# The weight sums of a Strassen product moved from VectorE to GpSimd, in a fused attention and MLP kernel

## The chip, the core and the metric

The kernel runs on one core of a Trainium2 chip. The metric is the device time of one launch in microseconds; lower is better. Engines are named as the profile names them: PE is TensorE's matmul, PEld its weight load, DVE is VectorE, ACT is ScalarE, POOL is GpSimd, SP is SyncE.

## The reference

Attention with a sliding window of 128 and a linear bias per head, over 8 batches, 8 heads, 576 positions and a head size of 64. Its output, as 4608 tokens of 512 columns, goes through two matrix products with a squared ReLU between them.

```
rel   = pos[:, None] - pos[None, :]
mask  = (rel >= 0) & (rel < 128)
s     = where(mask, scale * q @ k.T - slope[h] * |rel|, -1e9)
x     = (softmax(s) @ v)            as [4608, 512]
h     = x @ w_in                    w_in  [512, 2048]
out   = (relu(h) ** 2) @ w_out      w_out [2048, 512], float32
```

## The kernel before, in words

**Attention** is worked off in blocks of 128 keys, five to a batch, the last of 64 (40 blocks, counted here from 0, so that block 14 has 64 rows). For each block POOL issues three loads that also cast to bf16: k and q into a slot of `kq` (a ring of 4) and v into a slot of `vt` (a ring of 6). A slot is loaded again only when its last reader is done. For blocks up to 11 PE turns k and q; from block 12 on SP does it with a transposing DMA, kqT<-kq (L461, L463). PE then makes the scores (ps_s, L533 and L552), ACT the exponential (E, L598), DVE the mask (P, L609), PE the product with v (pv, L639), DVE the division (x, L672), and x is turned into `xT`, a ring of four groups of 512 tokens. The scores of blocks 14 and 15 are one step of PE.

**The MLP** takes the tokens in nine groups of 512. Group 0 is plain. Groups 0 and 1 form h by plain products (L745); groups 2 to 8 form h by Strassen's method in the form of Winograd, seven products of halves in place of eight, in four units of 512 columns of w_in each (`fast_unit`, L820). That needs four sums of w_in per unit, `w_sum`, which are formed once (`weight_sums`, L383 to L394) and used by all later groups, and four sums of the tokens per group. The second matrix product of groups 1 to 8 is formed the same way in seven products (`product`, L975), on sums of g and of w_out. In the last group its last product is done in two halves of 128 tokens each, so that the first can be added and stored while the second is still on PE (`halves`, L970, L1010 to L1022).

**The order of the work** is set by a planner (`Plan.order`). Each task has a cost on each engine that may do it, a key and what it depends on. The planner goes through time; of the tasks that could start soonest on an engine it takes the one with the lowest key. An engine then executes its list in this order and waits where something is not yet there. `SPREAD` (L1099) moves the keys by random draws: a seed, the largest move, and the share of the tasks that are moved (a negative share moves the loads).

Of the kernel before, what the change touches and what calls it, by code (L numbers as in the profile page):

```python
# [12 lines left out]
ALU = mybir.AluOpType  # L13
# [188 lines left out]
def kernel(  # L202
    ctx: ExitStack, tc: tile.TileContext, q, k, v, moe_w_in, moe_w_out, out
):
    nc = tc.nc
# [11 lines left out]
    FCB = d_ff // 128  # L217
    NG = NT // 512
# [41 lines left out]
    def overlap(e):  # L260
# [88 lines left out]
    t_win = [None] * 4  # L349
# [33 lines left out]
    def weight_sums(n, key):  # L383
        w = w_in_sb.rearrange("p (c k) (j r f) -> p c r k j f", c=2, r=2, f=128)
        a11, a12, a21, a22 = (w[:, c, r, :, 2 * n:2 * n + 2] for r in range(2) for c in range(2))
        s1, s2, s3, s4 = (w_sum[:, i, :, 2 * n:2 * n + 2] for i in range(4))
        last = None
        for o, a, b, op in ((s1, a21, a22, ALU.add), (s2, s1, a11, ALU.subtract),
                            (s3, a11, a21, ALU.subtract), (s4, a12, s2, ALU.subtract)):
            def emit(o=o, a=a, b=b, op=op):  # L390
                for k in range(2):
                    nc.vector.tensor_tensor(o[:, k], a[:, k], b[:, k], op=op)
# [333 lines left out]
    g_slots, g_sq, t_read = {}, {}, {}  # L726
# [215 lines left out]
    KEEP = {}  # L942
    BOTH = (2, 5)

    def left(g, what, j):
        if what == "s2":
            return s_slots[g][1].tile[:, j]
        if what in ("s1", "s4"):
            return s_slots[g][0].tile[:, ("s1", "s4").index(what), j]
        a11, a12, a21, a22 = quarters(g, j, 1)  # L950
        return {"a11": a11, "a12": a12, "s3": a21, "a22": a22}[what][:, 0]

    def right(what, j):
        if what[0] == "t":
            return w_mix[:, int(what[1]) - 1, j]
        return w_out_sb[:, 2 * j + int(what[1]) - 1, (int(what[2]) - 1) * 256:int(what[2]) * 256]

    def product(g, i, key):
        what, by, where = PRODUCTS[i]
        if i == 0:  # L960
            KEEP[g] = {"bank": [[Slot("o")] * 2, [Slot("o")] * 2, [Slot("o"), Slot("o")] if g == NG - 1 else [Slot("o")] * 2],
                       "last": None, "t": [None] * 3,
                       "s1": Slot("s1"), "u2": Slot("u2"), "x1": Slot("x1")}
        kp = KEEP[g]
        bank = kp["bank"][where]
# [4 lines left out]
        for j, t in ([(j, t) for t in range(2) for j in range(FCB // 2)] if halves  # L970
                     else [(j, t) for j in range(FCB // 2) for t in range(2)]):
                def emit(j=j, t=t):
                    if opens and j == 0 and (t == 0 or apart):
                        bank[t].tile = bank_tile(bank[t], "o")
                    nc.tensor.matmul(bank[t].tile[:, t * 256:(t + 1) * 256],  # L975
                                     left(g, what, j)[:, t * 128:(t + 1) * 128], right(by, j),
                                     start=opens and j == 0 and (t == 0 or apart), stop=j == FCB // 2 - 1,
                                     skip_group_check=True)
                new = j == 0 and t == 0
                here = [bank[t]] if opens and j == 0 and (t == 0 or apart) else []  # L980
                end = i == 6 and j == FCB // 2 - 1 and t == 1
                if halves and j == 0 and t == 1:
                    half_done = last
# [4 lines left out]
                last = plan.add({"PE": mm(256)}, key(i * 16 + 2 * j + t), emit,  # L988
                                [last, (t_wmix if by[0] == "t" else t_wout)[j // 2], kp["t"][where] if new else None] + needs,
                                here, [g_slots[g], s_slots[g][0]] if end else [s_slots[g][1]] if i == 1 and j == FCB // 2 - 1 and t == 1 else [])  # L990
        kp["last"] = last
        k = key(i * 16 + 15)

        def f32(tag, sl, n):
            sl.tile = work.tile([128, 512], FP32, tag=tag, bufs=n, name=tag)
            return sl.tile

        free = [bank[0]] if i in (2, 5, 6) else []
        if i in (0, 1, 2, 3, 5):
            so = {0: kp["s1"], 1: kp["u2"], 3: kp["x1"]}.get(i) or Slot("osb")  # L1000
            done_ = last
            if i == 1:
                def into():
                    nc.vector.tensor_tensor(bank[0].tile, bank[0].tile, kp["s1"].tile, op=ALU.add)
                done_ = plan.add({"DVE": dve(512)}, k, into, [last, kp["from", "s1"]], [], [kp["s1"]])

            def keep():
                copy(te, f32(so.tag, so, plan.bufs[so.tag]), bank[0].tile)
            te = plan.add({"ACT": act(512), "DVE": dve(512)} if i in BOTH else {"ACT": act(512)}, k, keep, [done_], [so], free)
        elif halves:  # L1010
            for t, dep in ((0, half_done), (1, last)):
                so = Slot("osb")

                def plus(t=t, so=so):
                    nc.vector.tensor_tensor(f32("osb", so, plan.bufs["osb"])[:, 0:256], bank[t].tile[:, t * 256:t * 256 + 256],
                                            kp["u2"].tile[:, t * 256:t * 256 + 256], op=ALU.add)
                te = plan.add({"DVE": dve(256)}, k, plus, [dep, kp["from", "u2"]], [so], [bank[t], kp["u2"]])

                def store(t=t, so=so):
                    r0 = g * 512 + t * 128  # L1020
                    nc.sync.dma_start(out[r0:r0 + 128, 256:512], so.tile[:, 0:256])
                plan.add({"SP": 350.0}, k, store, [te], [], [so], dma=1040.0)  # L1022
            return
        else:
            so = Slot("osb")
            add = kp[{4: "x1", 6: "u2"}[i]]

            te = None
            for lo, hi in ((0, 256), (256, 512)) if apart else ((0, 512),):
                def plus(lo=lo, hi=hi):  # L1030
                    if lo == 0:
                        f32(so.tag, so, plan.bufs[so.tag])
                    nc.vector.tensor_tensor(so.tile[:, lo:hi], bank[lo // 256].tile[:, lo:hi], add.tile[:, lo:hi], op=ALU.add)
# [35 lines left out]
    key = 0  # L1069
# [5 lines left out]
    for g in range(NG):  # L1075
# [27 lines left out]
    shift = dict.fromkeys(work_of + load_of, 0.0)  # L1103
# [53 lines left out]
```

## Time and profile before

| | |
|---|---|
| runs shown, us | 291.15, 291.99, 292.82 (median 291.99) |
| the profiled execution, us | 291.18 |
| its span, first to last instruction | 289.2 us |
| granted TensorE clock | 1.00 |
| PE busy | 281.6 us, 97% |
| DVE busy | 256.1 us, 89% |
| ACT busy | 229.1 us, 79% |
| POOL busy | 107.6 us, 37% |

The time of an execution is a little longer than its span, 291.18 against 289.2 us. Busy time of PE is the time in which matmuls run; they overlap, so that a matmul's own duration (273 ns for 256 columns) is longer than the step from one to the next. In a row of the timeline the columns are start, duration, engine, line, operation, destination and source and, in brackets, idle time before it and what ended it. In a list of waits they are the sum, the count and the longest. In the table of stretches they are the stretch, its length, busy time and instructions of PE, PEld, DVE, ACT and POOL, the granted clock, the share of the DMA engines and GB/s.

### The profile page before, as it was taken

To read this page: it belongs to the slowest core of one execution; us is meant where nothing else is said; L and a number is where in the kernel's file an instruction comes from. 1 tells how busy PE (TensorE), PEld (TensorE's weight loads), DVE (VectorE), ACT (ScalarE), POOL (GpSimd) and SP (SyncE) were. 2 spreads that over 40 slices of the span, in tenths; PEclk is the share of its full clock that TensorE was granted. 3 is DMA by queue.
4 is the path that set the end of the run, shared out by engine and by line. 5 is a ranking of instruction groups with operands and counts; after the bars stand their busy time and mean duration, and the time that the engine had idled before them with its cause. 6 is when DMAs were issued, how large, how long until landed. Compare 5 with 4: busy or idle time off the path is not lost.

```text
span 289.2 us, 9480 instructions
## 1 busy us (share of the span) xinstructions
PE 281.6 (97%) x3869; PEld 239.2 (83%) x3869; DVE 256.1 (89%) x625; ACT 229.1 (79%) x470; POOL 107.6 (37%) x134
## 2 busy tenths in 40 slices
PE   8899999999999999999999999999999999999995
PEld 6788878865788888888988888888888888888884
DVE  6876879999798999998999999989999988998823
ACT  6659888995489985999899989898879888588420
POOL 8958676944672516332634245332000000000000
PEclk9999999999999999999999999999999999999999
DMA  9999999999999999999999999999234101201223
GB/s 135 160 179 174 172 180 186 155 126 208 191 191 141 150 126 192 161 161 110 226 158 126 127 197 157 164 177 158 37 101 70 47 20 61 86 0 39 74 75 109
DMA packets 165867, 38.36 MB, mean 133 GB/s; under 512 B 153024, under 2 KB 165312, under 8 KB 165824
## 3 DMA queue, kind: packets, MB, share of 16 engines
q0 software_dynamic: 114704, 18.10, 92.3%
q1 hardware_dynamic: 50064, 19.41, 35.8%
q8 instruction: 30, 0.49, 0.7%
q10 hardware_dynamic: 1056, 0.26, 0.4%
q14 instruction: 13, 0.11, 0.1%
HBM read 36.70 MB, written 9.44 MB: 160 GB/s over the span
## 4 chain that ended last, share of the span: by engine, by line
PE 88%; POOL 4%; DMA 3%; DVE 2%; ACT 1%; issue 0%; DVEq 0%
PE o L975 33%; PE f L820 30%; PE h L745 8%; PE pv L639 6%; PE o L1054 5%; DMA w_in_sb<-in_moe_w_in_dram 3%; PE ps_s L533 3%; POOL kq L429 2%; PE ps_s L552 2%; POOL vt L429 1%; PE tp L483 1%; POOL w_in_sb L360 1%; PE xp L698 1%; DVE rt L854 1%; DVE g L869 0%
## 5 line engine op out<-in xcount | busy, mean ns | idle before, releaser
L429 POOL DMA_DIRECT2D vt<-in_v_dram x40 | 34.1, 854 | 66.5 <-PE pv L639 58.1
L598 ACT ACTIVATE E<-ps_s 128x384 bf16<-128x384 f32 (+2 forms) x114 | 50.5, 508 | 8.6 <-PE ps_s L533 8.6
L975 PEld LDWEIGHTS <-g 128*128 128x128 bf16 x512 | 49.1, 98 | 6.0
L820 PEld LDWEIGHTS <-w_sum 128*128 128x128 bf16 x448 | 43.1, 97 | 6.3 <-issue 0.5
L609 DVE TENSOR_TENSOR P<-E,masks 128x1024 bf16<-128x1024 bf16 (+1 forms) x67 | 43.5, 656 | 2.5 <-ACT E L598 1.6
L429 POOL DMA_DIRECT2D kq<-in_k_dram x39 | 33.2, 851 | 24.9 <-DMA kqT<-kq 17.5
L975 PEld LDWEIGHTS <-S 128*128 128x128 bf16 x384 | 36.6, 98 | 4.5 <-issue 0.4
L848 ACT ACTIVATE rt<-f 128x512 bf16<-128x512 f32 x56 | 33.2, 600 | 6.8 <-PE f L820 6.6
L975 PE MATMUL o<-w_out_sb,g 128*128 128x256 bf16 x256 | 38.3, 273 | 0.0
L975 PE MATMUL o<-w_mix,g 128*128 128x256 bf16 x256 | 37.2, 273 | 0.0
L745 PE MATMUL h<-xT,w_in_sb 128*128 128x128 bf16 (+1 forms) x384 | 35.3, 237 | 1.2 <-issue 0.6
L975 PE MATMUL o<-w_mix,S 128*128 128x256 bf16 x256 | 36.1, 273 | 0.2 <-ACT E L598 0.2
L820 PEld LDWEIGHTS <-w_in_sb 128*128 128x128 bf16 x336 | 31.8, 97 | 4.4
L820 PE MATMUL f<-xT,w_in_sb 128*128 128x256 bf16 x224 | 34.6, 273 | 0.0
L429 POOL DMA_DIRECT2D kq<-in_q_dram x39 | 33.4, 857 | 2.6 <-PE h L745 1.3
L871 ACT ACTIVATE g<-rt 128x512 bf16<-128x512 bf16 x52 | 32.6, 634 | 1.7 <-DVE rt L859 0.9
L820 PE MATMUL f<-xT,w_sum 128*128 128x256 bf16 x224 | 33.5, 272 | 0.2 <-DVE rt L854 0.2
L672 DVE TENSOR_TENSOR x<-pv,rec 128x256 bf16<-128x256 f32 (+1 forms) x80 | 33.0, 415 | 0.4
L820 PE MATMUL f<-T,w_sum 128*128 128x256 bf16 x224 | 32.1, 273 | 0.0
L639 PE MATMUL pv<-vt,P 128*128 128x65 bf16 x576 | 30.8, 193 | 0.9 <-DVE P L609 0.9
L639 PEld LDWEIGHTS <-P 128*128 128x128 bf16 x576 | 25.7, 97 | 6.1 <-DVE P L609 2.0
L745 PEld LDWEIGHTS <-w_in_sb 128*128 128x128 bf16 x384 | 26.7, 98 | 3.7 <-issue 1.0
(78 smaller groups left out, 504.1 us busy)
## 6 DMA issues: line engine op xcount, KB each, us to landing
out_dram<-osb SPq DMA_DIRECT2D x35, 256.0 KB, 3.7
vt<-in_v_dram POOLq DMA_DIRECT2D x32, 128.0 KB, 5.5
kq<-in_k_dram POOLq DMA_DIRECT2D x31, 128.0 KB, 6.0
kq<-in_q_dram POOLq DMA_DIRECT2D x31, 128.0 KB, 6.3
w_out_sb<-in_moe_w_out_dram POOLq DMA_DIRECT2D x4, 512.0 KB, 9.6
w_in_sb<-in_moe_w_in_dram POOLq DMA_DIRECT2D x6, 256.0 KB, 7.9
kq<-in_k_dram POOLq DMA_DIRECT2D x8, 64.0 KB, 5.7
kq<-in_q_dram POOLq DMA_DIRECT2D x8, 64.0 KB, 6.2
```

The costliest lines, as they stand in the source:

```text
L429: nc.gpsimd.dma_start(o, src[b, :, kb * 128:kb * 128 + n, :].rearrange("h s d -> s h d"))
L533: nc.tensor.matmul(sl.tile[lo:lo + 64, at:at + w], k[rows, c, unit:unit + 64], own[rows, C + c, q0:q0 + w], start=True, stop=True)
L598: nc.scalar.activation(o, src, AF.Exp, bias=0.0, scale=scale)
L609: nc.vector.tensor_tensor(Pt[sP.idx][:, hs, p0:2, 0:n], e, masks[:, hs, p0:2, 0:n], op=ALU.mult)
L639: nc.tensor.matmul(slot_v.tile[:, hi * (D + 1):(hi + 1) * (D + 1)], Pt[sP.idx][:, place(h), part, :], vt[s_in[mk, "v"].idx][:, h, :], star ...
L672: nc.vector.tensor_tensor(xt[sx.idx][0:n, hf * 256:(hf + 1) * 256].rearrange("p (h e) -> p h e", h=4), pv[0:n, :, 0:D], srec.tile[0:n, :]. ...
L745: nc.tensor.matmul(slot.tile[:, f * w:(f + 1) * w], w_in_sb[:, cc, (fc + f) * 128:(fc + f + 1) * 128], xT[:, cc, g * 512 % RING + lo:g * 5 ...
L820: nc.tensor.matmul(bank[name].tile[:, jj * 256:jj * 256 + 256], w, m, start=opens and jj == 0 and k == 0, stop=k == 1, skip_group_check=True)
L848: nc.scalar.activation(srt.tile, bank[name].tile, AF.Relu, bias=0.0, scale=1.0)
L871: nc.scalar.activation(o, i, AF.Square)
L975: nc.tensor.matmul(bank[t].tile[:, t * 256:(t + 1) * 256], left(g, what, j)[:, t * 128:(t + 1) * 128], right(by, j), start=opens and j == ...
L1054: nc.tensor.matmul(bank.tile, g_slots[g].tile[:, fc, t * 128:(t + 1) * 128], w_out_sb[:, fc], start=fc == 0, stop=fc == FCB - 1)
```

## The change

The sixteen sums of w_in leave DVE and go to POOL. On DVE each was two instructions of 256 columns (one for each k); on POOL each is one of 512. Their cost for the planner is 1250 ns each. They stand in POOL's list between the loads, where the planner puts them. Products five and seven of the last group open three banks instead of two: tokens 0 to 127, and tokens 128 to 255 in two pieces of 128 columns. The last product is worked off piece by piece, with an addition and a store for each. `SPREAD` has two draws in place of eleven.

```
-                {"h": 3, "o": 3, "a": 4, "f": 5, "t": 3})
+                {"h": 3, "o": 3, "a": 4, "f": 5, "t": 3, "z": 1})
...
             def emit(o=o, a=a, b=b, op=op):
-                for k in range(2):
-                    nc.vector.tensor_tensor(o[:, k], a[:, k], b[:, k], op=op)
-            last = plan.add({"DVE": 2 * dve(256, 2)}, key, emit, [t_win[n][-1], last, t_read[1][0]])
+                nc.gpsimd.tensor_tensor(o, a, b, op=op)
+            last = plan.add({"POOL": 1250.0}, key, emit, [t_win[n][-1], last, t_read[1][0]])
...
-            KEEP[g] = {"bank": [[Slot("o")] * 2, [Slot("o")] * 2, [Slot("o"), Slot("o")] if g == NG - 1 else [Slot("o")] * 2],
+            KEEP[g] = {"bank": [[Slot("o")] * 2, [Slot("o")] * 2, [Slot("o"), Slot("o"), Slot("z")] if g == NG - 1 else [Slot("o")] * 2],
...
+        parts = [(0, 0, 256), (1, 0, 128), (1, 128, 256)] if apart else [(0, 0, 256), (1, 0, 256)]
...
+        for j, x in ([(j, x) for x in range(len(parts)) for j in range(FCB // 2)] if halves
+                     else [(j, x) for j in range(FCB // 2) for x in range(len(parts))]):
+                t, lo, hi = parts[x]
...
+                    nc.tensor.matmul(bank[x].tile[:, t * 256 + lo:t * 256 + hi],
+                                     left(g, what, j)[:, t * 128:(t + 1) * 128], right(by, j)[:, lo:hi],
...
-            for t, dep in ((0, half_done), (1, last)):
+            for x, (t, lo, hi) in enumerate(parts):
...
-                    nc.sync.dma_start(out[r0:r0 + 128, 256:512], so.tile[:, 0:256])
+                    nc.sync.dma_start(out[r0:r0 + 128, 256 + lo:256 + hi], so.tile[:, 0:hi - lo])
...
-            for lo, hi in ((0, 256), (256, 512)) if apart else ((0, 512),):
+            for x, (lo, hi) in enumerate(((0, 256), (256, 384), (384, 512)) if apart else ((0, 512),)):
...
-    SPREAD = ((78, 3, 1), (425, 16, 0.01), (451, 8, 0.01), (463, 8, 0.03), (537, 3, 0.1), (602, 1.5, -0.15),
-              (705, 3, 0.03), (1454, 16, 0.03), (1463, 3, -0.15), (1578, 3, 0.03), (1611, 3, 0.01))
+    SPREAD = ((9072, 3, 1), (9274, 8, 0.03))
```

Three places show how the lists move. The first is POOL's list from the loads of block 12 on (its k and q go to kq_71, its v to vt_75; the following blocks go to kq_72, kq_73, kq_74 and kq_71 again). Before:

```order
L429 DMA kq_71<-in_q_dram 128x8x64
L429 DMA vt_75<-in_v_dram 128x8x64
L429 DMA kq_72<-in_k_dram 128x8x64
L429 DMA kq_72<-in_q_dram 128x8x64
L429 DMA vt_76<-in_v_dram 128x8x64
L429 DMA kq_73<-in_k_dram 64x8x64
L429 DMA kq_73<-in_q_dram 64x8x64
L429 DMA kq_74<-in_k_dram 128x8x64
L429 DMA kq_74<-in_q_dram 128x8x64
```

And now:

```order
L428 DMA kq_71<-in_q_dram 128x8x64
L428 DMA vt_75<-in_v_dram 128x8x64
L391 TENSOR_TENSOR w_sum<-w_in_sb 128x2x256 x2
L391 TENSOR_TENSOR w_sum<-w_sum,w_in_sb 128x2x256
L428 DMA vt_76<-in_v_dram 128x8x64
L428 DMA kq_72<-in_k_dram 128x8x64
L428 DMA kq_72<-in_q_dram 128x8x64
L391 TENSOR_TENSOR w_sum<-w_in_sb 128x2x256
L391 TENSOR_TENSOR w_sum<-w_sum,w_in_sb 128x2x256
L428 DMA kq_73<-in_k_dram 64x8x64
L428 DMA kq_73<-in_q_dram 64x8x64
```

Three sums stand ahead of block 13's loads and two more ahead of block 14's. Up to q of block 16 there are twelve, and the last of the sixteen stands behind v of block 20.

The second place is DVE's list where the sums of g for group 1 (S, from the rows of g) stand beside the later sums of w_in. Before:

```order
L934 TENSOR_TENSOR S_1577<-S,g 128x1024
L392 TENSOR_TENSOR w_sum<-w_in_sb,w_sum 128x256 x2
L443 COPY xT<-xp 128x4x128
L934 TENSOR_TENSOR g<-g 128x4x256
L392 TENSOR_TENSOR w_sum<-w_in_sb 128x256 x2
L934 TENSOR_TENSOR S<-g,S_1577 128x1024
L392 TENSOR_TENSOR w_sum<-w_sum,w_in_sb 128x256 x2
L609 TENSOR_TENSOR P_85<-E_90,masks 128x1024
```

And now:

```order
L933 TENSOR_TENSOR S_1595<-S,g 128x1024
L442 COPY xT<-xp 128x4x128
L933 TENSOR_TENSOR g<-g 128x4x256
L933 TENSOR_TENSOR S<-g,S_1595 128x1024
L608 TENSOR_TENSOR P_85<-E_90,masks 128x1024 x2
```

The sums of w_in are gone, and the rest closes up.

The third place is the end of DVE's list, the additions of the last group (x and u are kept parts, osb is what is stored). Before:

```order
L1004 TENSOR_TENSOR o<-o,s_5951 128x512
L443 COPY osb<-o 128x512
L1033 TENSOR_TENSOR osb<-o,x_6009 128x256 x2
L443 COPY osb<-o 128x512
L1015 TENSOR_TENSOR osb<-o,u_5977 128x256 x2
```

And now:

```order
L1008 TENSOR_TENSOR o<-o,s_5939 128x512
L442 COPY osb<-o 128x512
L1037 TENSOR_TENSOR osb<-o,x_5999 128x256
L1037 TENSOR_TENSOR osb<-o,x_5999 128x128 x2
L442 COPY osb<-o 128x512
L1019 TENSOR_TENSOR osb<-o,u_5965 128x256
L1019 TENSOR_TENSOR osb<-o,u_5965 128x128 x2
```

The second addition of each of the two products has become two of 128 columns. From L391 on line numbers differ by one to four between the two kernels.

More of the change, by code (lines that the diff above doesn't have):

```diff
@@ L969, in product, with emit @@
         halves = i == 6 and g == NG - 1
[L970 to L977, printed above, removed]
+        parts = [(0, 0, 256), (1, 0, 128), (1, 128, 256)] if apart else [(0, 0, 256), (1, 0, 256)]
+        done_at = []
+        for j, x in ([(j, x) for x in range(len(parts)) for j in range(FCB // 2)] if halves
+                     else [(j, x) for j in range(FCB // 2) for x in range(len(parts))]):
+                t, lo, hi = parts[x]
+                def emit(j=j, x=x, t=t, lo=lo, hi=hi):
+                    if opens and j == 0 and (x == 0 or apart):
+                        bank[x].tile = bank_tile(bank[x], "o")
+                    nc.tensor.matmul(bank[x].tile[:, t * 256 + lo:t * 256 + hi],
+                                     left(g, what, j)[:, t * 128:(t + 1) * 128], right(by, j)[:, lo:hi],
+                                     start=opens and j == 0 and (x == 0 or apart), stop=j == FCB // 2 - 1,
                                      skip_group_check=True)
+                t = x
                 new = j == 0 and t == 0
                 here = [bank[t]] if opens and j == 0 and (t == 0 or apart) else []
-                end = i == 6 and j == FCB // 2 - 1 and t == 1
-                if halves and j == 0 and t == 1:
-                    half_done = last
+                end = i == 6 and j == FCB // 2 - 1 and t == len(parts) - 1
                 if what[0] == "s":
@@ L987, in product @@
                     needs = [q for lo, hi, q in g_sq[g][2 * j + (what != "a11")]]
-                last = plan.add({"PE": mm(256)}, key(i * 16 + 2 * j + t), emit,
+                last = plan.add({"PE": mm(hi - lo)}, key(i * 16 + 2 * j + t), emit,
                                 [last, (t_wmix if by[0] == "t" else t_wout)[j // 2], kp["t"][where] if new else None] + needs,
                                 here, [g_slots[g], s_slots[g][0]] if end else [s_slots[g][1]] if i == 1 and j == FCB // 2 - 1 and t == 1 else [])
+                if j == FCB // 2 - 1:
+                    done_at.append(last)
         kp["last"] = last
```

14 lines of the change are left out of this document (7 added, 7 removed).

## The prediction

> **What bounds the kernel now.** I read the page's shares of the engines first, then PE's list of waits.
>
> ```profile
> PE 281.6 (97%) x3869; PEld 239.2 (83%) x3869; DVE 256.1 (89%) x625; ACT 229.1 (79%) x470; POOL 107.6 (37%) x134
> ```
> ```profile
> PE warm L310 <- DVE vt L338: 1.1, 1, 1.1
> PE pv L639 <- DVE P L609: 0.9, 2, 0.7
> PE h L745 <- issue: 0.6, 1, 0.6
> PE h L745 <- DMA w_in_sb<-in_moe_w_in_dram: 0.5, 1, 0.5
> PE ps_s L533 <- DVE kqT L443: 0.2, 1, 0.2
> PE o L975 <- ACT E L598: 0.2, 1, 0.2
> PE tp L483 <- DVE kq L443: 0.2, 1, 0.2
> PE f L820 <- DVE rt L854: 0.2, 1, 0.2
> ```
>
> PE is busy for 281.6 of 289.2 us, and all its waits together are 3.8 us. So PE is the bound. An engine that is relieved gains nothing unless PE waits for it; an engine that delays PE costs its delay in full, since PE has no idle time later to make it good. The chain of work puts one point of the start on a DMA:
>
> ```profile
> 12.96 9.18 DMA w_in_sb<-in_moe_w_in_dram
> 22.18 1.52 PE h L745 x23
> ```
>
> At 22.18 PE goes on because the third quarter of w_in has landed. The loads up to that one stand in the same order before and after, and in both orders 96 of the h products stand ahead of this wait. So I let PE start from 22.18 in both, and ask only what differs behind it.
>
> **The sums leave DVE.** The part of the trace in question is where w_sum is formed.
>
> ```profile
> L392 DVE TENSOR_TENSOR w_sum<-w_in_sb x16: 251/283/285, 47.5 to 70.2; 128x256 bf16<-128x256 bf16 x16
> L392 DVE TENSOR_TENSOR w_sum<-w_sum,w_in_sb x8: 279/282/285, 52.3 to 69.1; 128x256 bf16<-128x256 bf16 x8
> L392 DVE TENSOR_TENSOR w_sum<-w_in_sb,w_sum x8: 259/282/284, 54.5 to 71.3; 128x256 bf16<-128x256 bf16 x8
> ```
> ```profile
> 52.00:58.00 6.00, 6.00 (x89) 4.78 (x87) 6.00 (x27) 5.75 (x13) 5.46 (x7) 1.00 2.43 156
> ...
> sum 35.00, PE 35.00 PEld 25.24 DVE 32.45 ACT 27.25 POOL 20.39; mean PE 5.83 PEld 4.21 DVE 5.41 ACT 4.54 POOL 3.40
> ```
>
> Thirty-two instructions of 0.28 us are 9.0 us less on DVE between 47.5 and 71.6 us. The second fence is the table of stretches over 47 to 82 us: PE was busy in all 35.00 us, so DVE, though busy for 32.45, kept nobody waiting there. I cost the removal at **nothing**; PE's own work hides it.
>
> **The sums come to POOL.** In the same 35 us POOL is busy for 20.39, so 14.6 are idle. Sixteen sums of 512 columns come in. No row shows one. The nearest is POOL's only computing instruction on a wide tile:
>
> ```profile
> L288 POOL IOTA dist<- 128x256 f32 x1 | 0.3, 343 | 0.4 <-POOLq L1141 0.4
> ```
>
> It writes 256 columns in 343 ns, 1.34 ns a column. A sum reads two operands and writes one. If the three streams ran side by side, 512 columns would take 0.69 us; one after the other, 2.06 us. Those are the ends. I take the middle, two reads in turn with the write beside them: c = **1.37 us**, an estimate. Sixteen make 22 us, for which 14.6 us of idle are there. So the loads behind them become late, and the question is by how much.
>
> ```profile
> 50.95 0.88 POOL L429 DMA_DIRECT2D vt<-in_v_dram  x1
> 51.82 0.89 POOL L429 DMA_DIRECT2D kq<-in_k_dram  x1
> ...
> 54.41 0.73 POOL L429 DMA_DIRECT2D kq<-in_k_dram  x1
> 55.09 0.74 POOL L429 DMA_DIRECT2D kq<-in_q_dram  x1
> ...
> 65.16 0.90 POOL L429 DMA_DIRECT2D kq<-in_q_dram  x1
> ```
>
> The first row is v of block 12; behind it the first three sums now stand. From there on POOL worked without a break for five loads, 0.87 us from start to start for 128 rows and 0.68 for 64. Before block 16's q (65.16 in the trace) the changed order has twelve sums, eight loads of 128 rows and three of 64. POOL reaches it at 51.82 + 8 x 0.87 + 3 x 0.68 + 12c = 60.8 + 12c. For block 15's q it is four and two loads and seven sums: 56.7 + 7c. With c = 1.37 these are 77.3 and 66.2 us, 12.1 and 9.0 us later than before (57.25 for block 15's q).
>
> **What waits for these loads.** SP turns k and q into kqT, and PE's score products read that. The load of block 16 and the turning have these times to landing (tile kq in 64 to 66.5 us; all turns):
>
> ```profile
> DMA to landing us min/median/max: 5.8/5.8/6.3
> ```
> ```profile
> kqT<-kq SPq DMA_TRANSPOSE x28, 5.6
> ```
>
> So kqT is there 11.4 us after the issue of q. PE's scores of blocks 14 and 15, and of 16, began at
>
> ```profile
> 77.23 0.20 PE L552 MATMUL ps_s<-kqT,kqT 64*128 64x64 bf16 x2
> ```
> ```profile
> 86.42 0.24 PE L533 MATMUL ps_s<-kqT,kqT 64*64 64x128 bf16 x1
> ```
>
> In the changed order nine matmuls of 256 columns fewer stand ahead of the first and six fewer ahead of the second (four filler matmuls more, all before 22.18 us). A matmul of 256 columns takes 109 ns, from the 16 between these two starts:
>
> ```profile
> 282.03 1.91 PE L975 MATMUL o<-w_mix,g 128*128 128x256 bf16 x16
> 283.77 1.91 PE L975 MATMUL o<-w_out_sb,S 128*128 128x256 bf16 x16
> ```
>
> PE therefore comes to them at 76.25 and 85.77. Block 15: 66.2 + 11.4 = 77.6, a wait of 1.4 us. Block 16: 77.3 + 11.4 = 88.7, a wait of **2.9 us** in all, which contains the first. In general block 16's wait is 12c - 13.55: none below c = 1.13, 11.2 at the upper end. Later blocks have more room: for block 17 two sums and three loads are added, 2 x 1.37 + 3 x 0.87 = 5.4 us, and its scores stand 6.6 to 7.1 us behind those of 16.
>
> The sums themselves are in time. PE first reads one at 76.7, in the order of the quarters, while POOL has those of the first quarter by 64 us; for the last quarter the distance is about 10 us.
>
> ```profile
> L820 PE MATMUL f<-T,w_sum x224: 269/273/282, 76.7 to 266.1; 128*128 128x256 bf16 x112
> ```
>
> **The last product in three pieces.** In products five and seven of the last group eight matmuls of 256 columns each become sixteen of 128. Those step by 56 ns (twelve in 0.84 us, of which the last takes 0.22), so each product grows by 8 x (112 - 109) = 24 ns, 0.05 us in both.
>
> ```profile
> 33.58 0.84 PE L745 MATMUL h<-xT,w_in_sb 128*128 128x128 bf16 x12
> ```
> ```profile
> L1004 DVE TENSOR_TENSOR o<-o,s 128x512 f32<-128x512 f32 x8 | 5.5, 690 | 1.7 <-PE o L975 1.7
> ...
> L1015 DVE TENSOR_TENSOR osb<-o,u 128x256 f32<-128x256 f32 x2 | 0.8, 424 | 0.6 <-PE o L975 0.6
> ```
> ```profile
> 285.30 1.22 SPq L1021 DMA_DIRECT2D out_dram<-osb  x2
> 285.72 0.42 DVE L1015 TENSOR_TENSOR osb<-o,u 128x256 f32<-128x256 f32 x1 [0.45 <-PE o L975]
> ```
>
> Additions of 512 and 256 columns take 690 and 424 ns, so one of 128 takes about 290, and the last ends 0.13 us earlier. A third store queues on SP; its issue would stand at about 286.1, the second's of before at 286.2, so nothing is lost. A last store of half the bytes saves between nothing and 0.2 us. I take **-0.1 us** for it all.
>
> **The new draws** change the order on all engines. Beyond the two places above I cost them at nothing: at most the 2.3 us of PE's waits that neither the warm-up nor w_in accounts for can go, and new ones of that size can come.
>
> **The sum**, against the profiled execution's own 291.18 us: 291.18 + 2.9 - 0.1 = **294.0 us**. The median of the runs shown is 0.8 us above that execution; I leave the forecast on it, since its trace carries the sum.
>
> **The rivals.**
>
> *The loads arrive in time* (the other side: not slower). One mechanism, the price of a sum. Below c = 1.13 block 16 waits for nothing and the time is 291.1; up to c = 1.25 the wait stays under 1.46 us, 0.5%, which is about what a measurement of this kernel can tell from no change. For it speaks that SP turned block 16 at 71.60 and PE read it at 86.42, a room of 9 us; against it that twelve sums use this room up at 0.75 us each.
>
> ```profile
> 71.60 1.76 SPq L461 DMA_TRANSPOSE kqT<-kq  x1
> ```
>
> I give it 0.30. The Trainium skill, "GPSIMD Engine Reference", section 3.1, states 4497 ns for an addition of 2048 fp32 columns on GpSimd; a quarter is an estimate of 1.12 us, and by that the time would be 291.1. No run here shows it yet.
>
> *The draws take up PE's waits.* If the 2.3 us go and the loads are in time, 291.18 - 2.3 - 0.1 = 288.8. Against it: these waits are short ones in many places. 0.10.
>
> *DVE and POOL hinder each other.* Most of DVE's remaining work at 49 to 72 us is of two SBUF operands, such as
>
> ```profile
> L609 DVE TENSOR_TENSOR P<-E,masks 128x1024 bf16<-128x1024 bf16 x7 | 4.7, 674 | 0.0
> ```
>
> If a sum cannot start while such an instruction runs, it waits for half of one, 0.34 us, c becomes 1.71, block 16's wait 7.0 us and the time 298.1. DVE would wait for sums too, but has 9.0 us less to do. For it: DVE is nearly without a pause there. Against it: no row shows POOL computing beside DVE. 0.12. The Trainium skill, "SBUF — State Buffer", section "SBUF: two separate sides", says that DVE and GpSimd share a port pair as an exclusive lock, held for a whole instruction, by two-input DVE operations too against a GpSimd operation that reads SBUF. By that rule this rival is the case.
>
> **How the numbers follow.** The forecast has 0.48. Slower is it and the third rival, 0.60; same is the first, 0.30; faster the second, 0.10. The range leaves out the second rival and what lies above c = 1.71: 290.6 to 298.1. The forecast's own reaches from c = 1.25 to 1.5, 292.6 to 295.6.
>
> **What would show it.** In the changed profile the sums' duration on POOL (1.37); POOL without idle time from 52 to about 85 us; q of block 16 issued near 77 instead of 65; waits of PE at the score products at 76 and 86 us, 2.9 in all; the last addition near 290 ns. If PE does not wait there, the price of a sum or the time to landing is wrong; if it waits elsewhere for DVE, the third rival or the draws.

## The result, and the profile after

The changed kernel takes 306.97 us (median of 306.34, 308.6, 307.6 and 305.44) where the kernel before took 291.75 beside it on the same chip: a ratio of 1.052, 95% interval 1.0486 to 1.0555. It is slower, as forecast, but by five times as much as forecast, and outside the range. The profiled execution took 306.34 us, its span is 304.6. Times here and below are medians of all executions; the ratios leave out two slow ones (310.73 us in the kernel with broken rows, 294.61 us in the last one).

I read the same views as before. The page's shares of the engines and its chain of work by engine, and below them the chain of the kernel before:

```profile
PE 284.7 (93%) x3882; PEld 240.5 (79%) x3889; DVE 269.1 (88%) x597; ACT 228.2 (75%) x468; POOL 127.5 (42%) x150
...
PE 63%; DVE 26%; ACT 6%; issue 2%; DMA 1%; ACTq 0%; DVEq 0%
```
```profile
PE 88%; POOL 4%; DMA 3%; DVE 2%; ACT 1%; issue 0%; DVEq 0%
```

DVE has 28 instructions fewer, the sums among them, and is yet busy for 13.0 us more (269.1 against 256.1). A quarter of the chain that ended last is now on DVE, where it was 2%. PE's longest waits between 52 and 83 us say the same:

```profile
PE ps_s L551 <- DVE kqT L442: 4.0, 1, 4.0
PE pv L638 <- DVE P L608: 2.8, 1, 2.8
PE xp L697 <- DVE x L671: 1.6, 1, 1.6
```

None in this part is for a load. The table of stretches of the same part (in each row, behind the five engines, the granted clock, the DMA engines' share and GB/s):

```profile
52.00:58.00 6.00, 3.25 (x47) 2.69 (x44) 6.00 (x3) 3.84 (x9) 5.98 (x7) 1.00 1.63 105
58.00:65.00 7.00, 5.57 (x52) 4.17 (x54) 5.09 (x8) 3.03 (x6) 7.00 (x9) 0.76 1.45 112
65.00:72.00 7.00, 4.78 (x69) 3.10 (x69) 7.00 (x12) 6.16 (x13) 7.00 (x8) 1.00 1.32 122
72.00:77.00 5.00, 3.80 (x25) 1.97 (x25) 4.97 (x8) 0.00 (x0) 2.21 (x3) 0.66 0.44 56
77.00:82.00 5.00, 3.25 (x48) 1.69 (x48) 5.00 (x6) 1.60 (x4) 4.49 (x5) 1.00 1.01 107
sum 30.00, PE 20.65 PEld 13.62 DVE 28.05 ACT 14.63 POOL 26.68; mean PE 4.13 PEld 2.72 DVE 5.61 ACT 2.93 POOL 5.34
```

PE worked in 20.65 of 30.00 us, so 9.35 us went idle here; before it was busy in all of them. Twice the clock fell to 0.5 for 3.41 us (the 0.76 and the 0.66), each time behind a wait of PE. At half clock 3.41 us do the work of 1.7, so the two cost 3.4 us. 9.35 + 3.4 = 12.8 us of the 15.4 by which the span grew lie in this part. The first row shows where to look: DVE is busy for all 6.00 us with three instructions, where before it did 27. Here they are, and POOL's list beside them:

```profile
52.31 4.95 DVE L377 TENSOR_TENSOR w_mix<-w_out_sb 128x512 bf16<-128x512 bf16 x1
57.18 1.37 DVE L377 TENSOR_TENSOR w_mix<-w_out_sb,w_mix 128x512 bf16<-128x512 bf16 x1
```
```profile
52.01 0.88 POOL L428 DMA_DIRECT2D vt<-in_v_dram  x1
52.90 2.27 POOL L391 TENSOR_TENSOR w_sum<-w_in_sb 128x512 bf16<-128x512 bf16 x2
55.12 1.15 POOL L391 TENSOR_TENSOR w_sum<-w_sum,w_in_sb 128x512 bf16<-128x512 bf16 x1
56.21 0.91 POOL L428 DMA_DIRECT2D vt<-in_v_dram  x1
```

A subtraction that took 0.42 us just before takes 4.95, from within a load issue over three sums to the end of the next issue (57.12). It began 0.59 us before the first of the sums. DVE is not slow here, it stands still. Behind it in DVE's list stands the copy of kqT for which PE then waits 4.0 us. The sums themselves were cheaper than I took them for:

```profile
L391 POOL TENSOR_TENSOR w_sum<-w_in_sb x8: 1157/1182/1640, 52.9 to 92.5; 128x512 bf16<-128x512 bf16 x8
```

And the loads are late, much as forecast (q of blocks 15 and 16, forecast at 66.2 and 77.3):

```profile
65.84 0.89 POOL L428 DMA_DIRECT2D kq<-in_q_dram  x1
...
79.44 0.88 POOL L428 DMA_DIRECT2D kq<-in_q_dram  x1
```

Yet PE does not wait for them. DVE has held it up so long that it comes to the scores of block 16 at 100.50 us, where it came at 86.42 before, and goes on without idle time:

```profile
100.50 0.24 PE L532 MATMUL ps_s<-kqT,kqT 64*64 64x128 bf16 x1
```

So there were two theories to tell apart. **Standstill**: POOL's sums stop DVE's instructions on SBUF, PE waits for DVE. **Late loads**: the mechanism of the prediction. Others: the new draws, and the three pieces.

### The profile page after: what moved, and what is told of

It is laid out like the page before. It is cut to its first block, busy times and chain, and to the rows that moved or that the text cites. A ratio compares the mean times of both kernels' runs of the same rounds, so it can differ in the third digit from the quotient of the medians.

```text
span 304.6 us, 9499 instructions
## 1 busy us (share of the span) xinstructions
PE 284.7 (93%) x3882; PEld 240.5 (79%) x3889; DVE 269.1 (88%) x597; ACT 228.2 (75%) x468; POOL 127.5 (42%) x150
## 4 chain that ended last, share of the span: by engine, by line
PE 63%; DVE 26%; ACT 6%; issue 2%; DMA 1%; ACTq 0%; DVEq 0%
PE o L978 23%; PE f L819 21%; PE h L744 7%; DVE S L933 5%; DVE P L608 5%; PE pv L638 4%; DVE w_mix L377 3%; DVE rt L853 3%; DVE x L671 3%; PE ps_s L532 2%; PE o L1058 2%; ACT E L597 2%; DVE rt L858 1%; DMA raw<-in_q_dram 1%; PE tp L482 1%
## 5 line engine op out<-in xcount | busy, mean ns | idle before, releaser
L978 PEld LDWEIGHTS <-g 128*128 128x128 bf16 x512 | 48.4, 98 | 5.9
L608 DVE TENSOR_TENSOR P<-E,masks 128x1024 bf16<-128x1024 bf16 (+1 forms) x67 | 45.9, 693 | 1.7 <-ACT E L597 1.2
L978 PE MATMUL o<-w_mix,S 128*128 128x256 bf16 (+1 forms) x264 | 38.5, 269 | 0.0
L978 PE MATMUL o<-w_mix,g 128*128 128x256 bf16 x256 | 38.1, 273 | 0.0
L978 PE MATMUL o<-w_out_sb,g 128*128 128x256 bf16 x256 | 37.5, 273 | 0.0
L819 PE MATMUL f<-xT,w_in_sb 128*128 128x256 bf16 x224 | 36.3, 272 | 0.0
L819 PEld LDWEIGHTS <-w_in_sb 128*128 128x128 bf16 x336 | 32.5, 98 | 4.4 <-issue 0.3
L870 ACT ACTIVATE g<-rt 128x512 bf16<-128x512 bf16 x54 | 34.1, 639 | 1.9 <-DVE rt L858 1.3
L819 PE MATMUL f<-T,w_sum 128*128 128x256 bf16 x224 | 33.5, 273 | 0.4 <-ACT E L597 0.4
L744 PEld LDWEIGHTS <-w_in_sb 128*128 128x128 bf16 x384 | 27.2, 99 | 2.2 <-issue 0.2
```

What stands on the lines that cost most here:

```text
L608: nc.vector.tensor_tensor(Pt[sP.idx][:, hs, p0:2, 0:n], e, masks[:, hs, p0:2, 0:n], op=ALU.mult)
L744: nc.tensor.matmul(slot.tile[:, f * w:(f + 1) * w], w_in_sb[:, cc, (fc + f) * 128:(fc + f + 1) * 128], xT[:, cc, g * 512 % RING + lo:g * 5 ...
L819: nc.tensor.matmul(bank[name].tile[:, jj * 256:jj * 256 + 256], w, m, start=opens and jj == 0 and k == 0, stop=k == 1, skip_group_check=True)
L870: nc.scalar.activation(o, i, AF.Square)
L978: nc.tensor.matmul(bank[x].tile[:, t * 256 + lo:t * 256 + hi], left(g, what, j)[:, t * 128:(t + 1) * 128], right(by, j)[:, lo:hi], start=o ...
```

## The experiments

All ratios below are to the kernel before, run beside each on its chip; 1% is 2.9 us.

### The same order, the sums on DVE

```
-                nc.gpsimd.tensor_tensor(o, a, b, op=op)
+                for k in range(2):
+                    nc.vector.tensor_tensor(o[:, k], a[:, k], b[:, k], op=op)
```

> The changed kernel with its order of every engine kept and only the 16 sums emitted on DVE again, each as two instructions of 256 columns at the same place in the program; the new draws and the three pieces stay. DVE gets back 32 instructions of 0.28 us, 9.0 us. If the move is the cause (by DVE standing still, or by loads made late): the run comes back to 291 to 296 us, some 11 us or more below the changed kernel's 306.3, no DVE instruction of 128x512 bf16 takes over 0.7 us between 50 and 85 us, and the granted clock stays at 1.00 there. If the new draws or the three pieces are the cause: 303 us or more, with PE's waits still in place.

Measured: 293.67 us, ratio 1.0071 (1.0043 to 1.0100). In 52 to 58 us, DVE's groups by line:

```profile
L377 DVE TENSOR_TENSOR w_mix<-w_out_sb,w_mix 128x512 bf16<-128x512 bf16 x2 | 0.8, 422 | 0.0
L377 DVE TENSOR_TENSOR w_mix<-w_out_sb 128x512 bf16<-128x512 bf16 x2 | 0.8, 419 | 0.0
L392 DVE TENSOR_TENSOR w_sum<-w_in_sb 128x256 bf16<-128x256 bf16 x3 | 0.8, 287 | 0.0
```

The subtractions are back at 0.42 us although DVE has the sums too. With everything else of the change in place, 2.1 us of the loss are left; within this order the move to POOL makes 13.1.

### POOL held without reading SBUF

```
-                nc.gpsimd.tensor_tensor(o, a, b, op=op)
+                nc.gpsimd.memset(o, 0.03)
+                for k in range(2):
+                    nc.gpsimd.iota(scratch, pattern=[[-128, 2], [1, 128]], base=128, channel_multiplier=-1,
+                                   allow_small_or_imprecise_dtypes=True)
```

> The changed kernel in its own order, but each sum is replaced by a memset of its output and two IOTAs of 256 columns into a scratch tile on POOL: POOL is held for about as long (two IOTAs of 0.343 us each and a memset whose time no run here has shown, 0.8 to 1.5 us in all against the sum's 1.16 us), and reads no SBUF. It leaves out the sums of w_in: the products that use them are of a constant. If DVE stands still because POOL's sums hold what DVE reads through (my theory now): 291 to 296 us, 128x512 subtractions at 0.42 us, no half clock. If the late loads are the cause (the mechanism of my prediction): q of blocks 15 and 16 is issued as late as in the changed kernel (65.8 and 79.4 us) and the time stays at 304 us or more. If the draws are the cause: 304 us or more too, with loads early.

Measured: 297.62 us, ratio 1.0199 (1.0170 to 1.0229), between the two. POOL is held for 0.546 + 2 x 0.360 = 1.27 us a sum (medians and means of these):

```profile
L392 POOL MEMSET w_sum<- x16: 524/546/603, 51.9 to 89.6; 128x512 bf16 x16
```
```profile
L394 POOL IOTA scratch<- 128x256 f32 x32 | 11.5, 360 | 1.1
```

The page's shares of the engines:

```profile
PE 281.8 (95%) x3882; PEld 239.7 (81%) x3889; DVE 253.9 (86%) x597; ACT 228.1 (77%) x468; POOL 126.4 (43%) x182
```

DVE works off the same 597 instructions in 253.9 us of busy time, the changed kernel in 269.1: beside the sums they take 15.2 us more. Fills do not stop DVE. But PE now waits for what my prediction said, and at the first of the two places the clock falls to half for 3.41 us as well:

```profile
PE ps_s L536 <- DMA kqT<-kq: 4.5, 2, 2.7
```
```profile
97.00:102.00 5.00, 5.00 (x39) 3.93 (x38) 2.14 (x4) 3.10 (x8) 3.99 (x5) 0.69 1.74 195
```

So each mechanism can delay PE. The kernel with fills loses 5.8 us without a standstill, and sums in place of the fills, which do not read SBUF, cost 9.4 more. These are differences between kernels and not shares of the changed kernel's time: there PE waits for no late load, as said above, since it comes late itself. q of block 16 was issued at

```profile
76.28 0.88 POOL L432 DMA_DIRECT2D kq<-in_q_dram  x1
```

and 60.8 + 12 x 1.27 of my formula is 76.0.

### The fills cut to less than half

```
-                for k in range(2):
-                    nc.gpsimd.iota(scratch, pattern=[[-128, 2], [1, 128]], base=128, channel_multiplier=-1,
-                                   allow_small_or_imprecise_dtypes=True)
```

(against the kernel with fills)

> The run with fills on POOL, with the memsets alone: POOL is held 0.55 us for each sum in place of 1.27. It leaves out the sums of w_in, as that run does. My prediction's sum for late loads has no wait below 1.13 us for a sum. If the 3.9 us between the run with fills (297.6) and the sums on DVE in the same order (293.7) are late loads: no wait of PE for kqT over 0.5 us, no half clock, q of block 16 issued by 70 us, and 292 to 294 us. If they come from something else that fills do: 296 us or more.

Measured: 292.07 us, ratio 1.0022 (0.9994 to 1.0051); the clock stays at 1.00 and no wait for kqT is over 0.2 us. q of block 16:

```profile
67.30 0.90 POOL L428 DMA_DIRECT2D kq<-in_q_dram  x1
```

This shows three things. The wait for late loads is gone with POOL's hold at 0.57 us, so it was that. With DVE free of the sums, the new draws, the order and the pieces together cost 0.6 us (-0.2 to 1.5). And nothing stops DVE here, yet the kernel is not faster than the one before. But the same order with the sums on DVE had lost 2.1 us: within this order, where PE had several short waits for DVE, the relief is worth 1.4 us (0.3 to 2.6).

### The move alone, in the kernel before

The diff is that of the lines on the sums, from the change; draws and pieces are as before.

> The kernel before with its old draws and two pieces, and only the sums moved to POOL, planned as the change plans them. If the move is the cause: 301 to 310 us, with 128x512 subtractions of several us on DVE beside POOL's sums, and at least one stretch of PE at half clock after a wait. If the new draws are the cause: 291 to 295 us. Late loads alone would give 292 to 298.

Measured: 308.0 us, ratio 1.0560 (1.0505 to 1.0616). The old draws do not help: the move carries the loss alone. In its trace DVE's longest instructions beside the sums are of 3.28 us (128x512) and 4.80 us (128x1024), and PE is twice at half clock for 3.41 us.

### The three pieces alone

The kernel before with the three pieces only, first as they stand, then with the tasks' draws kept:

```
+    NEW = {t.group for t in plan.tasks if t.group[1] == 1220 and t.group[0].endswith("product.<locals>.emit")}
...
-    work_of = sorted({t.group for t in plan.tasks if t.group[1] > -100000})
+    work_of = sorted({t.group for t in plan.tasks if t.group[1] > -100000} - NEW)
```

> The kernel before with only the last product in three pieces. My prediction's term: 0.1 us less than before, 291.0 to 292.0 on the runs' scale and not to be told from it. If the third bank of the last group or the added 24 matmuls cost something that I did not see: over 293 us.

> The kernel before with the last product in three pieces, and with every task's draw as before: the three pieces make a new group of tasks (key 1220), by which each random draw after it falls on another task; here that group takes no part in the drawing, and the order of every engine is that of the kernel before up to the last product. My prediction's term for the pieces, 0.1 us less, 291.0 to 292.0 us on the runs' scale. If the 2.5 us of the run with three pieces and the old draws came from the pieces themselves: 294 us. If they came from the draws' falling on other tasks: back at the time of the kernel before, within 0.6 us.

Measured: 294.39 us, ratio 1.0089 (1.0062 to 1.0116), and with the draws kept 291.36 us, ratio 0.9979 (0.9964 to 0.9995). My first expectation missed: the pieces make one more group of tasks, so that each draw behind it in the list goes to another task, and this deal has a wait that the kernel before does not have:

```profile
PE ps_s L533 <- DMA kqT<-kq: 2.2, 1, 2.2
PE pv L639 <- issue: 1.6, 1, 1.6
```

The pieces themselves gain 0.6 us (0.1 to 1.1), and the last addition takes what I had worked out:

```profile
286.72 0.74 DVE L1020 TENSOR_TENSOR osb<-o,u 128x256 f32<-128x256 f32 x2 [0.18 <-PE o L979]
287.61 0.29 DVE L1020 TENSOR_TENSOR osb<-o,u 128x128 f32<-128x128 f32 x1 [0.15 <-PE o L979]
```

### Half of the sums on POOL

```
-                nc.gpsimd.tensor_tensor(o, a, b, op=op)
+                if n >= 2:
+                    nc.gpsimd.tensor_tensor(o, a, b, op=op)
+                    return
+                for k in range(2):
+                    nc.vector.tensor_tensor(o[:, k], a[:, k], b[:, k], op=op)
```

> The changed kernel's order with the first eight sums (n 0 and 1) on DVE at their place, as two instructions of 256 columns, and the last eight on POOL. In the changed kernel DVE's instructions beside the first eight sums took 9.8 us more than their usual time, beside the last eight 6.4. If each sum on POOL takes its time from DVE and, through it, from PE (theory now), about half of the 13.3 us between the two kernels of this order is left: 298 to 302 us. If only the first row of three sums (the subtraction of 4.95 us, PE's wait of 4.0 and the half clock behind it) decides: 294 to 297. If any sum on POOL sets the whole loss off: 304 or more.

Measured: 300.09 us, ratio 1.0275 (1.0235 to 1.0315): 8.0 us over the kernel before where all sixteen cost 15.2. The first row of three sums is on DVE here, and another row does the same to a sum of g (0.68 us usually) and through it to PE:

```profile
69.23 3.92 DVE L937 TENSOR_TENSOR S<-g,S 128x1024 bf16<-128x1024 bf16 x1
```
```profile
PE xp L701 <- DVE x L675: 3.0, 1, 3.0
```

With none, eight and sixteen sums on POOL this order loses 2.1, 8.0 and 15.2 us. So the first row of three sums does not hold the loss alone, and about half of the sums bring about half of it; other counts, or the other eight, were not tried.

### What stops what: the two engines by themselves

Three kernels in which DVE and POOL do one thing each, side by side.

> No attention and no products: nine stretches in which DVE does one kind of instruction back to back (128x512) while POOL does something beside it from about 2 us on; the output is a constant. (1) subtractions with two bf16 inputs in SBUF, alone; (2) the same beside six sums in a row; (3) beside six sums with three IOTAs between each two; (4) beside memsets and IOTAs; (5) additions of a bank and an SBUF tile beside six sums in a row; (6) copies of a bank; (7) copies from SBUF to SBUF; (8) subtractions beside 24 sums of 128 columns in a row; (9) subtractions beside six load issues. If DVE stands still while POOL's sums read SBUF: in (2) DVE finishes at most 4 of the 16 subtractions that fit into the six sums, with one instruction of 2 us or more; none is longer than 0.6 us in (1), (4), (5) and (6). If it is a run of sums that keeps DVE out, (3) shows at most one sum's time (1.2 us) on any one subtraction; if any sum does, each of the six does. If POOL's sums do not hinder DVE at all, (2) to (8) have the means of (1) within 10%. For (7), (8) and (9) I have no firm expectation; the trace of the changed kernel showed subtractions of 1.37 us beside load issues after sums.

It showed a direction that I had not looked for. DVE's subtractions kept 0.42 us each, and POOL's first sum took 7.95 us in place of 1.15: it was held until the row of thirty was through.

```profile
L35 DVE TENSOR_TENSOR d<-x,w x30: 418/419/425, 16.7 to 26.4; 128x512 bf16<-128x512 bf16 x30
```
```profile
19.87 7.95 POOL L48 TENSOR_TENSOR p<-y,w 128x512 bf16<-128x512 bf16 x1 [19.43 <-ACT y L91]
```

Beside additions of a bank and an SBUF tile neither waited, and a sum that nothing holds takes 1.16 us:

```profile
L38 DVE TENSOR_TENSOR fd<-bank,fs x20: 681/681/684, 72.5 to 83.9; 128x512 f32<-128x512 f32 x20
```
```profile
L48 POOL TENSOR_TENSOR p<-y,w x6: 1156/1158/1162, 76.3 to 81.9; 128x512 bf16<-128x512 bf16 x6
```

Since DVE began first in each stretch, the hold by POOL did not come up. In the second kernel POOL begins:

> As the run of prices alone, but POOL begins first and DVE joins some 2 us later; the output is a constant. (1) six sums in a row, DVE ten subtractions; (2) an IOTA after each sum; (3) a load issue after each sum; (4) six load issues, no sums; (5) six sums, DVE a subtraction and a copy of a bank in turn; (6) the same with DVE first; (7) six sums, DVE maxima of one SBUF input; (8) memsets and IOTAs on POOL; (9) a memset of one column after each sum. The run of prices alone showed a POOL sum wait 7.95 us until DVE's thirty subtractions in a row were through, and neither hinder the other where DVE read a bank. If whoever runs one such instruction behind another keeps the other out until its row ends (theory now): in (1) DVE's first subtraction ends after the sixth sum, 4 us or more after its start; in (2) and (9) DVE gets in behind the sum that runs, within 1.2 us, and all ten run through, while POOL's next sum waits 3.4 us for them; in (6) the sums get in behind the first subtraction and then hold DVE out. If it goes instruction by instruction, (1) would show ten subtractions of about 1.2 us each, and (2) and (9) as (1). In (3) and (4): if load issues hold DVE out too, subtractions of up to 0.9 us beside each issue; if not, 0.42. In (8): 0.42 throughout.

DVE got in behind the sum that ran, and from then on the two took turns, one subtraction to one sum:

```profile
6.31 1.36 DVE L35 TENSOR_TENSOR d<-x,w 128x512 bf16<-128x512 bf16 x1
```

1.36 us in place of 0.42, and the sums 1.33 in place of 1.15. Instead of "whoever runs in a row keeps the other out", only DVE's row had done so, in the first kernel; POOL's gave way at each sum. Nor did DVE's row always do it: in the stretch with load issues a sum that began beside running subtractions got in behind them and took 1.43 us. A memset of one column between sums changed nothing in the turns; an IOTA there let a second subtraction of 0.41 us through each time. Beside load issues without sums, subtractions kept their time:

```profile
L35 DVE TENSOR_TENSOR d<-x,w x10: 415/416/424, 51.8 to 54.8; 128x512 bf16<-128x512 bf16 x10
```

But a subtraction that began in a load issue between sums took 2.56 us. By that a break in POOL's rows might help, which I tried in the kernel itself:

```
                 nc.gpsimd.tensor_tensor(o, a, b, op=op)
+                nc.gpsimd.memset(tiny, 0.0)
```

> The changed kernel with a memset of one column (0.10 us in the page of the kernel before) behind each of POOL's sums, so that no two sums run in a row; POOL gets 16 times 0.10, 1.6 us. If DVE stands still because sums in a row keep it out for the whole row: no subtraction of 128x512 over 1.7 us in place of the 4.95, the first wait of PE for kqT (4.0 us) shrinks below 1.5 us, and the time falls by 4 us or more, to 297 to 303. If each sum takes its 1.16 us from DVE however it stands: the time stays within 1.5 us of 307 or grows by the 1.6 us. If the loads' lateness decides: it grows by 1 to 2 us.

Measured: 305.58 us, ratio 1.0452 (1.0395 to 1.0510). That theory fell: the same subtraction still stands for three sums, though not for the issue behind them,

```profile
51.62 4.29 DVE L377 TENSOR_TENSOR w_mix<-w_out_sb 128x512 bf16<-128x512 bf16 x1
```

and by the ratios the time comes down by 2 us, not by 4 or more. The last kernel puts POOL's rows and load issues in the order that they have in the change:

> DVE alone beside POOL, as in the two runs of prices, with POOL's order as in the changed kernel: two load issues, three sums in a row, two issues, two sums, two issues (in the third stretch: a sum, an issue, a sum, two issues, three sums). DVE joins in the first issues with (1) 40 subtractions, (2) subtractions and copies of a bank in turn, (3) subtractions, (4) maxima of one SBUF input. It is to settle what the first hold of the changed kernel was (4.95 us from within a load issue over three sums to the end of the next issue), which a memset of one column behind each sum did not shorten much (4.30 us). If POOL takes hold ahead of its sums, while the issue before them runs, and lets go only behind the issue after them: one subtraction of 4 to 5 us in (1) and (3), beginning in an issue, and in (3) holds of one sum and its issues, 2 to 3 us. If DVE gets in behind each sum as in the first run with POOL first: none over 1.5 us. If DVE's row keeps POOL out as in the run of prices: no subtraction over 0.45 us, and POOL's first sum waits for the end of DVE's row.

The long hold appears with the two engines alone, DVE above, POOL below:

```profile
5.20 3.85 DVE L35 TENSOR_TENSOR d<-x,w 128x512 bf16<-128x512 bf16 x1 [2.08 <-ACT x L106]
```
```profile
4.74 3.36 POOL L51 TENSOR_TENSOR p<-y,w 128x512 bf16<-128x512 bf16 x3
8.05 1.79 POOL L54 DMA_DIRECT2D l<-in_v_dram  x2
```

From 5.20, in the first sum, to 9.05, behind the first issue: 3.85 us for a subtraction of 0.42. Behind it the two took turns again at 1.36 us. When DVE gets in behind one sum and when only behind the row stays open: subtractions that began 0.25 and 0.33 us before a sum's end got in behind it, those that began 0.48 and 0.70 us before one, with two more sums right behind, did not. Yet in the turns subtractions began 1.08 us before a sum's end and got in. In the kernels themselves four long holds begin in the load issue ahead of a row of sums, 0.56 to 0.79 us before its first sum (4.95 and 4.04 us in the changed kernel, 4.29 with broken rows, 3.92 with half of the sums), and one of 4.80 us, in the move alone, 0.06 us behind the first sum's start.

### The version that the runs point to

The kernel before with the three pieces and the draws kept is the one version measured under both kernels (291.36 us, above). One step more on it, the sums on DVE as one instruction of 512 columns each:

```
-                for k in range(2):
-                    nc.vector.tensor_tensor(o[:, k], a[:, k], b[:, k], op=op)
+                nc.vector.tensor_tensor(o, a, b, op=op)
```

> The better version that the runs point to: the kernel before with the last product in three pieces and every task's draw kept (291.36 us, 0.6 less than the kernel before), and each sum of w_in on DVE as one instruction of 512 columns in place of two of 256, at the same place. DVE saves 16 times (2 x 0.28 - 0.42) = 2.2 us, which PE's work covers in the kernel before: 290.8 to 291.6 on the runs' scale, not to be told from the run with the pieces alone, and under the kernel before by some 0.2%.

Measured: 291.52 us, ratio 0.9988 (0.9965 to 1.0010): not to be told from the kernel before, nor from the version with the pieces alone. In this order what is saved on DVE is worth nothing that these runs can tell.

## Why the prediction was wrong, point by point

**PE is the bound, and pays for delay in full**: right for the kernel before. 12.8 of the 15.4 us are PE's own idle time and half clock in 52 to 82 us, and nothing of it was made good later. What the step lacked is that a wait can cost more than its length: behind two of the waits came 1.7 us each of half clock. And in this part of the changed kernel the chain of work runs mostly over DVE, so that the bound is DVE there.

**Removal from DVE at nothing**: right in that no kernel freed of the sums ran faster than the one before (the short fills, ratio 1.0022); within the changed order the removal is worth 1.4 us. The 9.0 us were too many, though: neighbours on DVE overlap, and the same order is busy for 258.7 us on DVE with the sums and for 253.2 without them, 5.5 us.

```profile
PE 281.1 (96%) x3882; PEld 238.3 (82%) x3889; DVE 258.7 (89%) x629; ACT 228.0 (78%) x468; POOL 107.7 (37%) x134
```
```profile
PE 281.3 (97%) x3889; PEld 239.0 (82%) x3889; DVE 253.2 (87%) x597; ACT 227.8 (79%) x468; POOL 115.5 (40%) x150
```

**A sum at 1.37 us**: too high; 1.16 unhindered, 1.33 in turns with DVE, 1.18 in the changed kernel. At 1.18 the forecast's formula gives a wait of 0.6 us, by which the time would have been the same as before. The lower estimate stood nearer: the 1.12 us that I took from the Trainium skill, "GPSIMD Engine Reference", section 3.1, differs from the 1.16 by 3%.

**Late loads, 2.9 us**: this is the term that made the forecast slower, and the changed kernel has no such wait, since DVE had held PE up before. So the direction came right by luck, through another mechanism. Where DVE is not stopped, in the run with fills, late loads do delay PE, and by more than the sum says. The issues came where the formula put them (76.3 for 76.0). With the hold of 1.27 us the formula gives 12 x 1.27 - 13.55 = 1.7 us of waits; measured were 4.5 us, the half clock behind one of them, and between the kernels with long and short fills 5.2 us. The waits were not at block 16, whose scores began at 86.51 without one, but at blocks 17 and 21, where I had written that later blocks have more room: the turning of block 17 was issued at 87.97 us and PE waited for it until 96.12, 8.1 us in place of the 5.6 that I had put for every one.

```profile
87.97 1.24 SPq L464 DMA_TRANSPOSE kqT<-kq  x1
```
```profile
96.12 0.24 PE L536 MATMUL ps_s<-kqT,kqT 64*64 64x128 bf16 x1 [2.66 <-DMA kqT<-kq]
```

**The third rival**, with its chance of 0.12, is where the prediction failed. It named the mechanism, with the Trainium skill's rule beside it, and then priced one side: a sum waits for half a DVE instruction. Of the other side it said: "DVE would wait for sums too, but has 9.0 us less to do." That is the step that fell: it put DVE's waits for the sums at nothing. DVE lost 15.2 us beside the sums (269.1 against 253.9, above; one subtraction 4.5 us of it) against 5.5 removed, and it lost them ahead of what PE needs next, in a stretch where it was busy for 32.45 of 35.00 us before. I had quoted that row as a sign that nobody waited for DVE; it was also the sign that a delay of DVE has nowhere to go. PE lost by it: 13.1 us against the same order with the sums on DVE, 9.4 against the same order with fills on POOL, which pay for late loads too.

The rule in the Trainium skill ("SBUF — State Buffer", section "SBUF: two separate sides") agrees in which instructions it concerns: two inputs in SBUF on DVE against a POOL operation that reads SBUF stop one another, one input from a bank does not (0.681 us beside sums). It has the loser wait for the instruction that holds; here one was held for a whole row (a sum took 7.95 us, a subtraction 4.95), and the measurement decides.

**Three pieces**: forecast -0.1, measured -0.6 (-1.1 to -0.1) with the draws kept; small either way. **New draws**: costed at nothing; with the order and the pieces they cost 0.6 us (-0.2 to 1.5) with DVE free of the sums. Dealing draws anew is not free of risk: the same old seeds on one task more cost 2.6 us. **The forecast's own span**: its bounds 292.6 and 295.6 leave out the -0.1 that the sum has; the formula gives 292.5 and 295.5.

## What to carry to other kernels

Before work is moved to POOL beside a busy DVE, price what it does to DVE's instructions on SBUF, not only what it takes on POOL: here each sum freed DVE of 0.34 us (5.5 in sixteen) and stopped it for 0.95 (15.2). An engine that is nearly full and feeds the bound is where a delay shows, though nobody waits for it yet. When seeds shuffle an order, keep each task's draw while testing an edit, or the shuffle is measured with it.

## What the runs showed of the hardware that was not expected

- A row of DVE's subtractions (128x512 bf16, two SBUF inputs, 0.34 us from start to start) stretched a POOL sum from 1.15 to 7.95 us, until the row ended; copies from SBUF to SBUF did the same, to 3.95 us. But sums that began beside subtractions in other stretches got in behind one or two of them (1.43 and 1.21 us). A row of POOL's sums mostly gave way after each sum, with 1.36 us for a subtraction and 1.23 for a maximum of one SBUF input (usually 0.28), but held one subtraction over three sums and a load issue (3.85 us, and 4.95 in the kernel, there begun 0.59 us before the first sum).
- Memsets and IOTAs on POOL, and load issues without sums, did not stretch subtractions (0.42 us beside each).
- The granted clock fell to 0.5 for 3.41 us at a time behind waits of PE of 3.96, 2.83 (changed kernel), 2.66 (fills) and 2.64 us (broken rows), and not behind waits of 2.2 (three pieces) or 3.0 us (half of the sums). So length alone does not decide. The changes of the clock stand whole multiples of 3.41 us apart in the traces (13.65 us between the two falls of the changed kernel, 10.24 in the move alone), so time can be cut into stretches of 3.41 us that end where a fall stands or could stand. In the stretch ahead of a fall amid the work PE was idle for 74 to 93%; of the stretches without a fall, between the start and the last matmuls, none was idle for more than 53%. The wait of 3.0 us lies across two stretches, idle for 45 and 44%. Here are the stretch ahead of the first fall in the changed kernel, the one at half clock, and the one ahead of the second fall; then the two of the wait of 3.0 us:

```profile
56.03:59.44 3.41, 0.23 (x8) 0.23 (x8) 3.41 (x4) 0.45 (x2) 3.41 (x5) 1.00 0.92 59
59.44:62.85 3.41, 3.19 (x24) 2.44 (x20) 2.47 (x2) 0.88 (x2) 3.41 (x5) 0.50 1.67 147
69.68:73.09 3.41, 0.69 (x7) 0.47 (x5) 3.41 (x5) 2.20 (x4) 2.91 (x2) 1.00 1.52 182
```
```profile
69.30:72.71 3.41, 1.89 (x11) 0.78 (x8) 3.41 (x2) 0.60 (x1) 3.39 (x4) 1.00 0.74 79
72.71:76.12 3.41, 1.90 (x40) 1.04 (x41) 3.41 (x7) 0.85 (x3) 2.38 (x3) 1.00 1.08 103
```

That the idle share of such a stretch decides fits every fall in these traces; no run was made to test it.
